# Sliding-window attention and a feed-forward layer on one core: three visits to small matmul tiles in a period instead of four

## The chip, the cores and the metric

The kernel runs on one core of one Trainium2 chip. Its engines work side by side, each through its own queue in order: TensorE (PE in the profile; PEld is its weight loads), VectorE (DVE), ScalarE (ACT), GpSimd (POOL), and SyncE (SP), which issues the DMAs. TensorE writes to PSUM, from where VectorE and ScalarE read. The metric is the time of one execution on the device in microseconds (us).

## What is computed

Attention with 8 heads over 576 positions for 8 batches, where half of the heads see the last 32 positions and half see every fourth of the last 128; its output, 4608 tokens of 512, goes through two matrices with a Gelu between. All data is float32.

```
scores = scale * q @ k.T                      # per batch and head, 576 x 576
mask_plain = (rel >= 0) & (rel < 32)
mask_dil = (rel >= 0) & (rel < 128) & (rel % 4 == 0)
attn = softmax(where(mask, scores, -1e9))     # heads 0-3 plain, heads 4-7 dilated
x = (attn @ v) as (4608, 512)
h = x @ w_in                                  # 512 x 2048
out = gelu(h) @ w_out                         # 2048 x 512
```

## The kernel before

The work is cut into 16 chunks, each half a batch: 288 tokens. A chunk c has four pairs of heads; pairs 0 and 1 are plain, pairs 2 and 3 dilated. The feed-forward products are large: 128 x 128 weights, 288 columns. To keep float32's accuracy in a faster format, each operand is held as a high and a low part (xh and xl, the two halves of win, wout and g), and each product is three matmuls.

Chunks 0 and 1 and the attention of chunk 2 are set in order by a planner (`Plan`), which this change does not touch. From chunk 2 on the order is written out (lines 604 to 653). One chunk's feed-forward is a period of 32 positions. Positions 0 to 15 are the first products: for each of 16 blocks f of the hidden size, 12 matmuls into one PSUM bank (ps_h, line 445), then Gelu and a copy on ScalarE and a residue on VectorE. Positions 16 to 31 are the second products: for each of 4 output blocks d, 16 x 3 matmuls into one bank (ps_o, line 459), then a copy by VectorE and a store. Position 16 + 4d + f/4 stands behind block f of output block d.

Into the period of chunk c-1 the attention of chunk c is sown. Each of its steps has a position and a rank in a table (lines 604 and 605, one entry for each pair); steps are sorted by position, then by rank, then as they were added, and `upto` emits what is due. All engines' queues follow that one order. The steps of a pair are:

- load (A_LOAD): q and k into raw_qk. The products' v comes for all pairs at A_V.
- scores (A_SC, line 310): small float32 matmuls, 64 rows by 32 columns of the array, 18 for a plain pair from here on and 24 for a dilated one, into half of each of two PSUM banks (ps_a).
- lowest (A_SC too, line 322): in three parts u, VectorE adds the mask, takes each row's minimum of the negated scores and moves them to sm.
- softmax (A_E, line 331): in three parts, six exponentials with sums on ScalarE, in place.
- norm and turn (A_N): VectorE divides (lines 352 to 361) and transposes (lines 371 and 376) into the tile turned.
- av and xout (A_X): the products with v (line 411), small matmuls on quarters of the array, 64 x 64, 18 or 24 a pair, into px_a; then ScalarE copies the high part xh (line 431) and VectorE forms the residue xl (line 434), which the next period's first products read.

A "visit" below is a place where TensorE leaves the large matmuls for these small ones. Two pairs share a PSUM tile of two banks, and tiles take turns on four banks (ps_a and px_a, a ring of two). A float32 matmul leaves two records in the trace, and two weight loads.

## Time and profile before

| | |
|---|---|
| median of 3 runs | 946.67 us (945.33 to 946.92) |
| the profiled execution | 945.82 us, span 944.0 us |
| granted TensorE clock, mean | 0.998 |
| TensorE busy | 916.4 us, 97% of the span |
| VectorE busy | 500.2 us, 53% |
| ScalarE busy | 435.4 us, 46% |
| chain that ended last | PE 96%; ps_h 44%, ps_o 44%, px_a 4%, ps_a 3% |

The chain that ended last is followed back from the last instruction, at each step to what released it. With 96% of it on TensorE, the other engines matter where TensorE waits for one of them, and the small matmuls matter by the time that they take TensorE away from the large ones. Matmuls are pipelined: a record lasts longer than the distance to the next one, and its end is modelled.

### The profile page before, as it was taken

The numbers are of one execution on the slowest core, as the hardware profiler recorded it, in microseconds if no ns is written. First come the engines' busy times: TensorE is split into PE (matmuls) and PEld (weight loads), VectorE is DVE, ScalarE is ACT, GpSimd is POOL, SyncE is SP. The second block draws the span as 40 slices with busy tenths as digits, with TensorE's granted clock in tenths as the row PEclk, the third lists the DMA queues.
The fourth block names the chain that finished last, engine by engine and source line by source line (L and its number), as shares of the span: only waits on it lengthen the run. The fifth ranks groups of instructions, "written<-read, shape, count | busy, mean of one in ns | idle before, by whom it ended". The sixth has DMA issues, their size and how long they took to land.

```text
span 944.0 us, 27638 instructions
## 1 busy us (share of the span) xinstructions
PE 916.4 (97%) x11632; PEld 898.6 (95%) x11632; DVE 500.2 (53%) x1957; ACT 435.4 (46%) x1398; POOL 21.0 (2%) x64
## 2 busy tenths in 40 slices
PE   4599999999999999999999999999999999999998
PEld 3499999999999999999999999999999999999998
DVE  6889974364635446354454635446354454635420
ACT  5535453634536245363634546255363634546240
POOL 1400020000000000000000000000000000000000
PEclk9999999999999999999999999999999999999999
DMA  9987233022040401204022040401204022040000
GB/s 319 405 297 261 92 126 137 4 78 75 8 145 8 132 17 51 103 8 145 2 82 71 8 146 8 138 9 60 93 8 145 2 86 68 13 139 8 21 1 26
DMA packets 34988, 83.69 MB, mean 89 GB/s; under 512 B 3888, under 2 KB 12080, under 8 KB 34864
## 3 DMA queue, kind: packets, MB, share of 16 engines
q1 hardware_dynamic: 34864, 81.93, 25.3%
q8 instruction: 91, 1.49, 0.7%
q14 instruction: 33, 0.27, 0.1%
HBM read 72.47 MB, written 9.44 MB: 87 GB/s over the span
## 4 chain that ended last, share of the span: by engine, by line
PE 96%; DMA 1%; issue 1%; DVE 1%; ACT 0%; SPq 0%
PE ps_h L445 44%; PE ps_o L459 44%; PE px_a L411 4%; PE ps_a L310 3%; DMA raw_qk<-qk_d 1%; PE px L395 1%; PE ps_sc L310 1%; DMA raw_w<-w_in 0%; DVE sm L322 0%; PE px L411 0%; DVE cv L199 0%; DVE sm L361 0%; ACT sm L331 0%; DVE cv L197 0%; DVE win L232 0%
## 5 line engine op out<-in xcount | busy, mean ns | idle before, releaser
L459 PE MATMUL ps_o<-g,wout 128*128 128x288 f32 x3072 | 420.1, 296 | 0.0
L459 PEld LDWEIGHTS ps_o<-g,wout 128*128 128x128 f32 x3072 | 409.7, 188 | 0.9
L445 PE MATMUL ps_h<-xh,win 128*128 128x288 f32 x1920 | 388.7, 297 | 0.0
L445 PEld LDWEIGHTS ps_h<-xh,win 128*128 128x128 f32 x1920 | 308.2, 188 | 2.8
L445 PE MATMUL ps_h<-xl,win 128*128 128x288 f32 x960 | 284.0, 296 | 0.0
L454 DVE TENSOR_TENSOR g<-gf,g 128x288 fp32r<-128x288 f32 x256 | 117.0, 457 | 259.2 <-ACT g L452 259.0
L449 ACT ACTIVATE gf<-ps_h 128x288 f32<-128x288 f32 x256 | 105.2, 411 | 297.6 <-PE ps_h L445 297.5
L445 PEld LDWEIGHTS ps_h<-xl,win 128*128 128x128 f32 x960 | 181.0, 189 | 0.0
L331 ACT ACTIVATE sm<-sm,st 128x64 f32<-128x64 f32 (+1 forms) x360 | 120.2, 335 | 12.5 <-DVE st L322 11.4
L452 ACT CAST g<-gf 128x288 fp32r<-128x288 f32 x256 | 111.0, 434 | 7.9
L431 ACT CAST xh<-px_a 128x256 fp32r<-128x256 f32 (+1 forms) x78 | 29.5, 413 | 132.7 <-PE px_a L411 84.8
L376 DVE STREAM_TRANSPOSE turned<-sm 32x192 f32<-32x192 f32 (+2 forms) x248 | 81.3, 328 | 6.2
L179 DVE COPY o_sb<-ps_o 128x288 f32<-128x288 f32 x58 | 26.4, 456 | 83.3 <-PE ps_o L459 82.4
L331 ACT ACTIVATION_READ_ACCUMULATOR sm<-sm,st 128x1 f32 (+1 forms) x360 | 67.2, 187 | 0.0
L434 DVE TENSOR_TENSOR xl<-px_a,xh 128x256 fp32r<-128x256 f32 (+1 forms) x78 | 31.3, 429 | 37.5 <-ACT xh L431 37.1
L322 DVE CUSTOM_DVE_ANT_0 sm<-ps_a,masks 128x64 f32<-128x64 f32 (+1 forms) x312 | 48.0, 216 | 0.6
L371 DVE STREAM_TRANSPOSE turned<-sm 128x256 f32<-128x256 f32 (+2 forms) x90 | 41.1, 457 | 9.0 <-POOL sm L358 4.2
L411 PEld LDWEIGHTS px_a<-turned,v_all 64*64 64x64 f32 x2184 | 35.6, 135 | 4.3 <-issue 4.3
L411 PE MATMUL px_a<-turned,v_all 64*64 64x32 f32 (+1 forms) x2184 | 38.2, 216 | 0.0
L361 DVE TENSOR_TENSOR sm<-sm,st 128x256 f32<-128x256 f32 (+2 forms) x82 | 35.1, 428 | 2.8
L352 DVE TENSOR_SCALAR st<-st 128x4 f32<-128x4 f32 (+2 forms) x90 | 14.2, 160 | 31.0 <-ACT sm L331 30.1
L310 PE MATMUL ps_sc<-raw_qk 64*32 64x64 f32 x504 | 12.3, 294 | 18.8 <-issue 8.4
(40 smaller groups left out, 392.8 us busy)
## 6 DMA issues: line engine op xcount, KB each, us to landing
raw_qk<-qk_d SPq DMA_DIRECT2D x32, 364.0 KB, 5.4
v_all<-v_p SPq DMA_DIRECT2D x28, 384.0 KB, 3.8
v_all<-v_d SPq DMA_DIRECT2D x28, 384.0 KB, 5.4
raw_qk<-qk_p SPq DMA_DIRECT2D x32, 304.0 KB, 4.2
outT<-o_sb SPq DMA_DIRECT2D x64, 144.0 KB, 1.8
raw_w<-w_in SPq DMA_DIRECT2D x16, 512.0 KB, 6.1
raw_w<-w_out SPq DMA_DIRECT2D x16, 512.0 KB, 5.7
mid_w<-w_out SPq DMA_DIRECT2D x10, 511.5 KB, 8.0
```

Of the source, the lines that this page charges most:

```text
L310: nc.tensor.matmul(s.sc[h][32 * r:32 * r + 32, u * 2 * KB:(u + 1) * 2 * KB], x[:, q0:q0 + 32], x[:, k0:k0 + 2 * KB], start=True, stop=True)
L322: nc.vector.tensor_tensor_reduce(out=s.sm[rs, i], in0=s.sc[h][rs, cols], in1=mask_of(s, u), scale=-SCALE, scalar=3.0e38, op0=ALU.add, op1= ...
L331: nc.scalar.activation(t, t, AF.Exp, bias=s.st[rs, 0, i:i + 1], scale=-1.0, accum_out=s.st[rs, 1, i:i + 1])
L361: nc.vector.tensor_mul(t, t, st.unsqueeze(2).broadcast_to((rs.stop - rs.start, 2 * (u1 - u0), 2 * KB)))
L371: nc.vector.transpose(s.t[rs, i].rearrange("p i j b -> p (i j b)"), s.sm[rs, i].rearrange("p i k -> p (i k)"))
L376: nc.vector.transpose(s.t[32 * to:32 * to + 32, i, r % 2], s.sm[32 * r:32 * r + 32, i, j * KB:(j + 1) * KB])
L411: nc.tensor.matmul(px[h * D:(h + 1) * D, r - r0, u * KB:u * KB + b], s.v[rows, u, j, h * D:(h + 1) * D], s.t[rows, 2 * u + h, j, 0:b], sta ...
L445: nc.tensor.matmul(ps, wins[f][:, t, cc * P:(cc + 1) * P], xx, start=(n == 0), stop=(n == 3 * NC - 1))
L449: nc.scalar.activation(gf, ps, AF.Gelu)
L452: nc.scalar.copy(g[:, 0], gf)
L454: nc.vector.tensor_sub(g[:, 1], gf, g[:, 0])
L459: nc.tensor.matmul(ps, wouts[f][:, t, d * P:(d + 1) * P], gs[f][:, u], start=(f == 0 and n == 0), stop=(f == NF - 1 and n == 2))
```

## The change

Two lines of the table, the rule for when a new PSUM tile is taken, the position of a pair's minima and one rank are changed. Scores of pairs 0, 1 and 2 stand at position 3 together, pair 3's at 22.25, behind the products of pairs 0 and 1, which move there from 22.5 and get rank 0. The products of pairs 2 and 3 move from 27 to 28. The minima of pairs 0 to 2 are spread over positions 3 to 11, one part at each; pair 3's follow its scores at once, and its exponentials, normalization and transposes move behind them. Pairs 0 and 1 share a score tile; pairs 2 and 3 take one each.

```diff
-    A_LOAD, A_V, A_SC, A_X = -6, 2, (3, 3, 9, 9), (22.5, 22.5, 27, 27)
-    A_E, A_N = (16.25, 16.5, 16.75, 17), (18.5, 20, 21.5, 23.25)
+    A_LOAD, A_V, A_SC, A_X = -6, 2, (3, 3, 3, 22.25), (22.25, 22.25, 28, 28)
+    A_E, A_N = (16.25, 16.5, 16.75, 22.5), (18.5, 20.25, 22, 25.5)
...
     def scores_of(s):
-        if s.p % 2 == 0:
+        if s.p != 1:
             banks["s"] = ps_a.tile([P, 2, 512], F32, tag="a", name="ps_a")
...
             for u in range(NU):
-                add(A_SC[p], 2, lowest(s, u))
+                add(A_SC[p] + (NU * p + u if p < 3 else 0), 2, lowest(s, u))
                 add(A_E[p], 3, softmax(s, u))
...
-            add(A_X[p], 6, av_of(s))
+            add(A_X[p], 0, av_of(s))
```

On TensorE, the second products of a period before, with the visits of pairs 0 and 1 and of pairs 2 and 3:

```order
L459 MATMUL ps_o<-g,wout 128x288 x81
L411 MATMUL px_a<-turned,v_all 64x32 x36
L459 MATMUL ps_o<-g,wout 128x288 x54
L411 MATMUL px_a<-turned,v_all 64x32 x16
L411 MATMUL px_a<-turned,v_all 64x8 x8
```

The same stretch of TensorE's queue now:

```order
L459 MATMUL ps_o<-g,wout 128x288 x78
L411 MATMUL px_a<-turned,v_all 64x32 x36
L310 MATMUL ps_a<-raw_qk 32x64 x24
L459 MATMUL ps_o<-g,wout 128x288 x69
L411 MATMUL px_a<-turned,v_all 64x32 x16
L411 MATMUL px_a<-turned,v_all 64x8 x8
```

The first of the two visits stands three large matmuls earlier and has pair 3's 24 score matmuls at its end; the second stands 12 further on. Among the first products, where visits of 36 and 48 score matmuls stood, one of 60 stands now, at the place of the first.

On VectorE before, from pair 1's last transposes on (the row of 128 x 384 is a dilated pair's):

```order
L371 STREAM_TRANSPOSE turned<-sm 32x128
L376 STREAM_TRANSPOSE turned<-sm 32x2x32
L352 TENSOR_SCALAR st<-st 128x6
L354 RECIPROCAL st<-st 128x6
L361 TENSOR_TENSOR sm<-sm,st 128x384
L371 STREAM_TRANSPOSE turned<-sm 128x384
L376 STREAM_TRANSPOSE turned<-sm 32x6x32 x4
L434 TENSOR_TENSOR xl<-px_a,xh 128x4x2x32
L434 TENSOR_TENSOR xl<-px_a,xh 128x32
```

VectorE from the same place now:

```order
L371 STREAM_TRANSPOSE turned<-sm 32x128
L376 STREAM_TRANSPOSE turned<-sm 32x2x32
L352 TENSOR_SCALAR st<-st 128x6
L354 RECIPROCAL st<-st 128x6
L361 TENSOR_TENSOR sm<-sm,st 128x384
L371 STREAM_TRANSPOSE turned<-sm 128x384
L376 STREAM_TRANSPOSE turned<-sm 32x6x32 x4
L322 ISA sm,st<-ps_a,masks 128x64
L322 ISA st 128x1
```

Pair 3's six minima (two rows each) have come between pair 2's transposes and the residues of pairs 0 and 1; all that stands ahead of pair 2's transposes is as before.

On ScalarE before, the exponentials of pairs 1 to 3 and the copies of the high parts:

```order
L331 ACTIVATE sm,st<-sm,st 128x64 x12
L431 CAST xh<-px_a 128x4x2x32
L431 CAST xh<-px_a 128x32
L431 CAST xh<-px_a 128x4x2x32
L431 CAST xh<-px_a 128x32
L431 CAST xh<-px_a 128x4x72 x2
```

And now:

```order
L331 ACTIVATE sm,st<-sm,st 128x64 x6
L431 CAST xh<-px_a 128x4x2x32
L431 CAST xh<-px_a 128x32
L431 CAST xh<-px_a 128x4x2x32
L431 CAST xh<-px_a 128x32
L331 ACTIVATE sm,st<-sm,st 128x64 x6
L431 CAST xh<-px_a 128x4x72 x2
```

Pair 3's six exponentials have moved behind the copies of pairs 0 and 1.

## Rows read from the trace of the kernel before

**Rows 1.** Chain of waits in order of time, one period, last chunk: start, length, what
```profile
437.44 6.37 PE ps_h L445 x48
...
444.74 9.75 PE ps_h L445 x72
...
465.37 10.71 PE ps_o L459 x81
476.08 1.30 PE px_a L411 x72
...
484.75 1.51 PE px_a L411 x96
...
494.02 6.37 PE ps_h L445 x48
...
889.80 25.49 PE ps_h L445 x192
```

**Rows 2.** Timeline of TensorE's matmuls at the second visit: start, length, instructions
```profile
454.20 0.29 PE L445 MATMUL ps_h<-xl,win 128*128 128x288 f32 x1
454.42 0.30 PE L310 MATMUL ps_a<-raw_qk 64*32 64x64 f32 x9
...
454.87 0.75 PE L310 MATMUL ps_a<-raw_qk 64*32 64x64 f32 x51
455.55 0.53 PE L445 MATMUL ps_h<-xh,win 128*128 128x288 f32 x2
```

**Rows 3.** Timeline of VectorE: minima of the first visit, pairs 1 and 2
```profile
444.75 0.46 DVE L454 TENSOR_TENSOR g<-gf,g 128x288 fp32r<-128x288 f32 x1 [1.13 <-ACT g L452]
445.13 0.22 DVE L322 CUSTOM_DVE_ANT_0 sm<-ps_a,masks 128x64 f32<-128x64 f32 x1
...
445.27 0.22 DVE L322 CUSTOM_DVE_ANT_0 sm<-ps_a,masks 128x64 f32<-128x64 f32 x1
...
476.78 0.24 DVE L376 STREAM_TRANSPOSE turned<-sm 32x64 f32<-32x64 f32 x1
477.05 0.17 DVE L352 TENSOR_SCALAR st<-st 128x6 f32<-128x6 f32 x1
...
478.69 1.56 DVE L376 STREAM_TRANSPOSE turned<-sm 32x192 f32<-32x192 f32 x4
480.28 0.52 DVE L434 TENSOR_TENSOR xl<-px_a,xh 128x256 fp32r<-128x256 f32 x2
```

**Rows 4.** Timeline of TensorE, third and fourth visit; last its loads by form
```profile
476.01 1.37 PE L411 MATMUL px_a<-turned,v_all 64*64 64x32 f32 x72
...
477.02 0.36 PE L411 MATMUL px_a<-turned,v_all 64*64 64x32 f32 x6
...
477.07 0.20 PEld L411 LDWEIGHTS px_a<-turned,v_all 64*64 64x64 f32 x4
...
477.31 7.44 PE L459 MATMUL ps_o<-g,wout 128*128 128x288 f32 x54
...
484.68 1.49 PEld L411 LDWEIGHTS px_a<-turned,v_all 64*64 64x64 f32 x96 [0.16 <-issue]
...
L411 PEld LDWEIGHTS px_a<-turned,v_all 64*64 64x64 f32 x168 | 2.8, 135 | 0.3 <-issue 0.3
```

**Rows 5.** Timeline of TensorE early in the kernel: products of chunk 0, then scores
```profile
39.38 0.51 PE L395 MATMUL px<-turned,v_sb 32*64 32x32 f32 x27
39.81 0.32 PE L310 MATMUL ps_sc<-raw_qk 64*32 64x64 f32 x8
```

**Rows 6.** ScalarE: timeline of pair 1's copy; exponentials of the period by form
```profile
480.83 0.46 ACT L431 CAST xh<-px_a 128x256 fp32r<-128x256 f32 x2 [2.95 <-DVE xl L434]
...
L331 ACT ACTIVATE sm<-sm,st 128x64 f32<-128x64 f32 x20 | 6.7, 334 | 0.0
```

**Rows 7.** DMA queue in the first period: timeline, then issues by line with time to landing
```profile
156.51 0.91 SPq L262 DMA_DIRECT2D raw_qk<-qk_d  x2
...
raw_qk<-qk_d SPq DMA_DIRECT2D x2, 364.0 KB, 5.4
```

## The prediction

> **What bounds the kernel now.** I read the share of the span by engine first: TensorE is busy for 97% of it and makes up 96% of the chain that ended last (the table above), so only what TensorE does, or waits for, is worth anything. Next I read that chain in order of time [rows 1]. It repeats a period of 56.58 us (437.44 to 494.02), thirteen times up to 889.80, once for the attention of each chunk from 3 to 15: a stretch of first products (ps_h) with two visits to small score tiles, then a stretch of second products (ps_o) with two visits to the attention products (px_a). The last chunk has no visits, and its ps_h stretch of 192 matmuls takes 25.49 us [rows 1], 0.133 us each. In a period the same stretch runs from 437.44 to 465.37, 27.93 us, so the two score visits cost 2.44 us together.

> That cost splits by visit. From 437.44 to 444.74 are 7.30 us, 6.37 of them for 48 large matmuls: 0.93 us. The 72 matmuls behind that visit take 9.75 us, where 72 x 25.49 / 192 is 9.56: they come 0.19 us late. So the first visit costs 1.12 us, and 1.32 are left for the second. Every small matmul leaves two records (fp32): the first visit has 72, the second 96, so 24 more records cost 0.20 us, 8.3 ns each, and a visit without records would still cost about 0.5 us. Within a visit the pace is uneven [rows 2]: the second starts 45 records in its first 0.45 us (454.42 to 454.87), and then 51 between 454.87 and 455.40 (end of the row less the 0.22 us that one lasts), 10.6 ns each.

> The third visit is already late in the kernel before. VectorE ends pair 1's last transpose at 477.02 (476.78 + 0.24) and goes on with pair 2 at 477.05 [rows 3]; the last four weight loads of pair 1's product begin at 477.07 [rows 4], 0.05 us behind it. In the fourth visit 96 loads take 1.49 us and one lasts 0.135 [rows 4]: 14.3 ns from one start to the next; at that pace the four would have begun 68 loads after 476.01, at 476.98. So the end of the third visit is set by VectorE and not by TensorE.

> **The change, part by part.**

> *Fewer visits among the first products.* The second visit goes, and pair 2's 48 records join the first. One visit of 120 records costs 1.52 us by the difference between visits (1.32 + 24 x 0.0083) and 1.63 us if the 48 run at the later pace (1.12 + 48 x 0.0106). I take 1.60, since records that join a running visit meet the later pace. The gain is 2.44 - 1.60 = 0.84 us a period, bounds 0.81 and 0.92.

> *Products of pairs 0 and 1 three matmuls earlier.* At 22.25 in place of 22.5, 78 large matmuls of the stretch are done and not 81. TensorE reaches the visit 3 x 0.133 = 0.40 us earlier, but what ends the visit is VectorE's transpose, and nothing moves that. In the order on VectorE the whole row from pair 0's normalization to pair 1's transposes, the first output copy between them, is the same, and ScalarE's softmax of pairs 0 and 1 is too; both start behind the last Gelu, which stands at a fixed distance from the start of the ps_o stretch. So the av matmuls end where they ended, and the three matmuls that used to lie under the wait come after it: a loss of 0.40 us a period. It would be a gain of nothing, and a loss of nothing, only if pair 1's transposes came 0.4 us sooner.

> *Pair 3's scores behind these products.* In the kernel before, the large matmuls resume at 477.31, which is 0.07 us ahead of the modelled end (477.02 + 0.36) of the last small one [rows 4]. The same 0.07 us shows where a visit begins (454.20 + 0.29 against 454.42 [rows 2]), and 0.08 us at a change from one small shape to another without a large one between, at the start of the kernel: 39.38 + 0.51 against 39.81 [rows 5]. So I start the scores at 477.31, as the large matmuls before. Their 48 records take some 0.48 us to start by the head of [rows 2] (bounds 0.40 and 0.51, at 8.3 and 10.6 ns), the last one ends 0.22 us on, and the large matmuls begin 0.07 us ahead of that: 477.93, 0.62 us later than before. If the change of shape cost nothing, the scores would begin some 0.13 us sooner; if it cost what a visit's beginning does (0.22 us from the start of the last matmul, [rows 2], against 0.15 here), 0.07 us later. [...] With a free change inside the visit the sum below would be +0.05 us a period in place of +0.18.

> *Sum for a period:* + 0.62 (scores of pair 3 here) + 0.40 (the three matmuls) - 0.84 (two visits into one) = +0.18 us. The bounds: 0.81 - 0.92 = -0.11 and 1.12 - 0.81 = +0.31 us (0.81 is 1.02 less 0.13 and 0.08, 1.12 is 1.02 plus 0.07 and 0.03).

> *VectorE's score minima spread over nine steps.* The bursts of twelve among the ps_h stretch become nine pieces of two. I cost it at nothing: VectorE idles 1.13 us ahead of a residue in that stretch, and two minima take 0.29 us (0.145 us apart, [rows 3]). If that cover were gone, Gelu would wait for its buffer and TensorE for a PSUM bank; shorter pieces make this less likely than before.

> *Pair 3's chain gets late.* Its minima, exponentials and transposes now lie between its scores and the last visit. VectorE is busy with pair 2 until 480.25 (478.69 + 1.56), and then, where it started pair 0's residue at 480.28 [rows 3], it takes six minima: 0.87 us, to 481.15. Pair 0's residue follows (0.52 us, to 481.67), and it alone lets ScalarE copy pair 1, as it did at 480.83, 0.03 us after that residue [rows 6]: 481.70 to 482.16. Behind that copy in ScalarE's queue stand pair 3's six exponentials, 334 ns each [rows 6]: to about 484.3 with the last read-out. Behind VectorE's wait for them stand the normalization and the transposes, 3.20 us as pair 2's (477.05 to 480.25): to 487.5. TensorE needs them when? From 477.93, 69 large matmuls take 9.36 us (69 x 0.1328 and 0.19), so the last visit begins at 487.3; pair 2 goes first with 48 records at 14.3 ns, 0.7 us: 488.0. The chain has some 0.5 us in hand, so I cost it at nothing. Residues of pairs 2 and 3, the output copies and the reload of Gelu's table end some microseconds ahead of the next ps_h stretch, which follows 45 matmuls (6 us) behind that visit.

> *Loads.* The order of the DMA queue does not change, and pair 3's tile is held for longer without a load that waits for it. Only in the first period are the loads issued close ahead: pairs 2 and 3 from 156.51, and they land 5.4 us later in the median [rows 7], at 161.9. The first visit reached its end at about 161.8; pair 2's scores now stand there. That may cost 0.2 us, once.

> **The time.** 13 x 0.18 = 2.3 us, with 0.2 for the load not added: the profiled execution of 945.82 us (span 944.04) becomes 948.2. It lies 0.85 us below the median of the runs, 946.67; carried over to that median the sum is 949.0 us. Bounds: 13 x -0.11 = -1.4 and 13 x 0.31 = +4.0, thus 945.2 to 950.7.

> **Rivals.**
> 1. *The visit saved is a plain gain.* If VectorE's transpose of pair 1 did not end the merged visit, the 0.40 would fall away and the period would be 0.22 us shorter: 13 x 0.22 = 2.9 us, 943.8 us. For it: a visit does cost 0.5 us however small it is. Against it: the 0.05 us between transpose and loads in [rows 3, 4], and an order on VectorE and ScalarE that is the same up to there. It decides from the point at which the transpose ends before about 476.6. 8%.
> 2. *Gain and loss cancel.* The change of shape costs little, the 48 records run at 8.3 ns in both places, and the sum lies between -0.11 and +0.05 us: about 946.3 us. For it: the records of small matmuls come in bursts, and [rows 5] are from the start of the kernel and another shape. 26%.
> 3. *Pair 3 comes late to the last visit.* Its chain runs through three engines with 0.5 us in hand; 0.9 us more on it would stop TensorE 0.4 us in each period, 5 us more than my sum: 954 us. For it: every link waits for another engine. Against it: every link has a duration from the trace. 7%.

> My forecast, a sum from +0.05 to +0.31 us a period, has 59%, and its own range is 947.3 to 950.7. With the cancelling case and some of the scatter of the runs (945.33 to 946.92), the range is 945.4 to 951.0. About 0.2%, 1.9 us, is what a measurement can tell from no change here. The forecast is beyond that from 0.15 us a period on, some four fifths of its chance: with rival 3, 54% slower; 8% faster; 38% for no change.

> **What would show it.** In the profile of the changed kernel: a ps_h stretch of about 27.1 us with one visit; a third-visit row in which the last four loads of pair 1's product still begin 0.05 us behind VectorE's transpose, about 11.8 us after the stretch's start, although the visit begins 0.4 us earlier; the scores starting 0.15 us behind the last product; large matmuls again 0.6 us later; and a last visit without a gap. The period should be 56.76 us. I am wrong if the merged visit ends earlier than VectorE lets it by this reading, if one visit of 120 records costs far from 1.6 us, or if TensorE idles in the last visit.

## The result, and the profile after

The changed kernel takes 949.79 us, median of 8 runs (948.45 to 952.09), against 945.52 us for the kernel before (8 runs, 944.74 to 948.31). The ratio is 1.0041, with a 95% interval of 1.0031 to 1.0051: slower by 0.41%, 2.9 to 4.8 us. The forecast was 949.0 us in a range of 945.4 to 951.0, slower, by a sum of 2.3 us. The runs of one kernel spread with the granted clock of TensorE, so equal clocks are compared too: at 0.998 the changed kernel takes 948.45 to 950.00 us (median of three 948.58), at 0.996 949.18 to 949.94 (949.63), at 0.994 951.62 and 952.09. The kernel before, in its runs beside the experiments below on two chips, has medians of 945.67 (34 runs), 946.23 (9) and 948.61 (5) at these clocks. That is 2.9 to 3.4 us less at each.

The chain of waits of the changed kernel in order of time (start, length, what); a period from 441.10 to 497.92 answers to [rows 1]:

```profile
157.11 6.37 PE ps_h L445 x48
...
441.10 6.38 PE ps_h L445 x48
447.48 1.44 PE ps_a L310 x92
448.92 19.31 PE ps_h L445 x144
468.23 10.31 PE ps_o L459 x78
478.54 1.36 PE px_a L411 x66
...
480.24 0.66 PE ps_a L310 x45
480.89 9.36 PE ps_o L459 x69
490.26 1.51 PE px_a L411 x96
491.77 6.15 PE ps_o L459 x45
497.92 6.37 PE ps_h L445 x48
...
895.59 25.49 PE ps_h L445 x192
```

Read it by stretches. From 441.10 to 468.23 are 27.13 us, where the kernel before has 27.93: 0.80 us are gained by one score visit in place of two, with pair 3's 48 records gone to the merged visit. From 468.23 to 480.89 are 12.66 us for 78 large matmuls and the merged visit; before, 81 large matmuls and the visit took 12.01 us (465.37 to 476.08 + 1.30). So the large matmuls resume 0.65 us later, and with three of them (0.40 us) still to do. The last visit takes 1.51 us as before. Sum: 0.65 + 0.40 - 0.80 = +0.25 us.

Over all thirteen periods, from the start of the first to the start of the last chunk's first products, it is 895.59 - 157.11 = 738.48 us. The kernel before starts them here, in its own chain:

```profile
154.66 6.37 PE ps_h L445 x48
```

889.80 - 154.66 = 735.14 us. The periods are 3.34 us longer, 0.26 each, which lies inside the interval of the runs. The span of this one profiled execution grew by more, 5.8 us (949.8 against 944.0): the other 2.45 us lie ahead of the first period, where both kernels have the same instructions in the same order. There the granted clock was at 0.50, with 1.00 ahead of it and behind it, from 47.38 to 57.62 us in this execution, and from 48.80 to 52.21 in that of the kernel before. Twelve large matmuls took 3.18 us at 0.50 (from 48.61) and 1.59 at 1.00 (from 62.11). TensorE was busy for 4.01 of the 6.83 us ahead of the one fall and for 6.30 of the 10.24 us ahead of the other. By its length the difference, 6.8 us more at half the pace, can hold the 2.45 us, but two other profiles with 3.41 us at the lower clock begin the first period at 153.91 and 155.25, so it need not be the clock alone. That start ended between 153.91 and 157.11 us in the profiles of kernels that share it, so comparisons below are made by the thirteen periods and by the runs, not by spans.

VectorE in the changed kernel (start, length, instruction): the end of pair 1's transposes, the second of the two residues of pairs 0 and 1, then pair 3's normalization and transposes:

```profile
479.64 0.24 DVE L376 STREAM_TRANSPOSE turned<-sm 32x64 f32<-32x64 f32 x1
...
485.00 0.52 DVE L434 TENSOR_TENSOR xl<-px_a,xh 128x256 fp32r<-128x256 f32 x2 [0.53 <-ACT xh L431]
...
486.99 0.17 DVE L352 TENSOR_SCALAR st<-st 128x6 f32<-128x6 f32 x1 [1.10 <-ACT sm L331]
...
488.62 1.55 DVE L376 STREAM_TRANSPOSE turned<-sm 32x192 f32<-32x192 f32 x4
```

TensorE's matmuls and loads in the same two visits:

```profile
478.47 1.77 PE L411 MATMUL px_a<-turned,v_all 64*64 64x32 f32 x72
...
479.93 0.30 PE L411 MATMUL px_a<-turned,v_all 64*64 64x32 f32 x4
480.17 0.34 PE L310 MATMUL ps_a<-raw_qk 64*32 64x64 f32 x16
...
490.18 1.49 PEld L411 LDWEIGHTS px_a<-turned,v_all 64*64 64x64 f32 x96 [0.17 <-issue]
```

Three things are to be seen. The 72 product records take 1.77 us where they took 1.37 [rows 4]: the visit begins 0.40 us earlier and does not end earlier. The last four begin at 479.93, 0.05 us behind VectorE's transpose (479.64 + 0.24), the distance of [rows 3, 4]. And the transpose ends 11.65 us behind the start of the ps_o stretch (479.88 - 468.23), as before (477.02 - 465.37). The granted clock was 0.994 over the span, 0.998 before; within the periods the large matmuls kept their pace (25.49 us for 192 in both).

### The profile page after: what moved, and what is told of

Same layout as the page of the kernel before. It is cut to its first block, busy times and chain, and to the rows that moved or that the text cites. A ratio compares the mean times of both kernels' runs of the same rounds, so it can differ in the third digit from the quotient of the medians.

```text
span 949.8 us, 27626 instructions
## 1 busy us (share of the span) xinstructions
PE 922.3 (97%) x11632; PEld 903.9 (95%) x11632; DVE 501.8 (53%) x1957; ACT 435.7 (46%) x1398; POOL 21.1 (2%) x64
## 3 DMA queue, kind: packets, MB, share of 16 engines
q8 instruction: 91, 1.49, 0.7%
## 4 chain that ended last, share of the span: by engine, by line
PE 96%; DMA 2%; issue 1%; DVE 0%; SPq 0%
PE ps_h L445 44%; PE ps_o L459 43%; PE px_a L411 4%; PE ps_a L310 3%; DMA raw_qk<-qk_d 1%; DMA mid_w<-w_out 1%; PE px L395 1%; DMA v_sb<-v_p 1%; PE ps_sc L310 0%; PE px L411 0%; DVE sm L322 0%; SPq L262 0%; DVE cv L199 0%; DVE o_sb L179 0%; DVE raw_w L203 0%
## 5 line engine op out<-in xcount | busy, mean ns | idle before, releaser
L322 DVE CUSTOM_DVE_ANT_0 sm<-ps_a,masks 128x64 f32<-128x64 f32 (+1 forms) x312 | 54.8, 219 | 1.0
L411 PEld LDWEIGHTS px_a<-turned,v_all 64*64 64x64 f32 x2184 | 37.7, 134 | 7.2 <-issue 4.2
L411 PE MATMUL px_a<-turned,v_all 64*64 64x32 f32 (+1 forms) x2184 | 42.9, 217 | 0.4
L322 DVE DVE_READ_ACCUMULATOR2_ANT st<- 128x1 f32 (+2 forms) x384 | 31.3, 81 | 0.0
```

The costliest lines, as they stand in the source:

```text
L322: nc.vector.tensor_tensor_reduce(out=s.sm[rs, i], in0=s.sc[h][rs, cols], in1=mask_of(s, u), scale=-SCALE, scalar=3.0e38, op0=ALU.add, op1= ...
L411: nc.tensor.matmul(px[h * D:(h + 1) * D, r - r0, u * KB:u * KB + b], s.v[rows, u, j, h * D:(h + 1) * D], s.t[rows, 2 * u + h, j, 0:b], sta ...
```

## Experiments

All ratios are to the kernel before, timed on the same chip.

**Scores first in the merged visit.** One rank of the changed kernel is put back.

```diff
-            add(A_X[p], 0, av_of(s))
+            add(A_X[p], 6, av_of(s))
```

> The changed kernel with one rank put back: in the merged visit at 22.25 pair 3's scores come ahead of the products of pairs 0 and 1, so TensorE works on them while VectorE ends pair 1's transposes. Theory (the loss is 0.40 us a period of waiting for that transpose, beside 0.66 us for pair 3's scores here, against 0.80 us saved among the first products): the scores fill the wait, the products end about 12.1 us after the start of the second products in place of 11.95, and a period is 0.25 us shorter than that of the kernel before: 13 x 0.25 = 3.3 us faster than before, some 6.6 us faster than the changed kernel. Rival (two shapes in one visit, or scores in that place, are what costs): the order inside the visit makes no difference, and it stays 3 to 4 us slower than before.

Measured: 943.56 us, ratio 0.9972 (0.9960 to 0.9983), 1.6 to 3.8 us faster than before. TensorE's matmuls in its merged visit, the second products having begun at 463.56:

```profile
473.83 0.72 PE L310 MATMUL ps_a<-raw_qk 64*32 64x64 f32 x48
474.49 1.25 PE L411 MATMUL px_a<-turned,v_all 64*64 64x32 f32 x72
475.67 0.40 PE L459 MATMUL ps_o<-g,wout 128*128 128x288 f32 x1
```

The products take 1.25 us in place of 1.77: their wait lies under the scores now. The thirteen periods take 732.57 us, 2.57 less than before. Twelve of them are 56.27 to 56.33 us long, 0.25 less than the 56.55 before, as expected; the one that begins at 717.93 takes 56.95, because TensorE stands still for 0.39 us ("issue") a few matmuls behind its score visit; the last section has the reason. The rival that the order inside the visit makes no difference is out: the same instructions in another order turn the loss into a gain. Of all versions run this is the fastest.

**Products three matmuls earlier, nothing else.** The kernel before with one number changed:

```diff
-(22.5, 22.5, 27, 27)
+(22.25, 22.25, 27, 27)
```

> The kernel before with one number changed: the products of pairs 0 and 1 at 22.25 in place of 22.5, three large matmuls earlier; four visits as before. Theory: the visit begins 0.40 us earlier and ends where it ended, since VectorE's transpose of pair 1 sets its end: 13 x 0.40 = 5.2 us slower than before. Rival (TensorE does not wait there, the visit takes its time whatever VectorE does): no change, within 1 us of before.

Measured: 950.51 us, ratio 1.0047 (1.0031 to 1.0063). Its chain of waits shows the visit in two pieces:

```profile
466.50 10.31 PE ps_o L459 x78
476.81 1.36 PE px_a L411 x66
...
478.20 0.30 PE px_a L411 x4
478.51 7.73 PE ps_o L459 x57
```

From 476.81 to 478.51 are 1.70 us where [rows 1] have 1.30: the 0.40 us that the visit came earlier. VectorE's last transpose of pair 1 there:

```profile
477.91 0.24 DVE L376 STREAM_TRANSPOSE turned<-sm 32x64 f32<-32x64 f32 x1
```

It ends at 478.15, and the last four records begin at 478.20. The thirteen periods are 4.95 us longer than before (740.09), 0.38 each. So this part of the change, alone, costs more than the whole of it (3.34).

**The merged visit at 22.5.** The changed kernel with the visit where the products stood before:

```diff
-(3, 3, 3, 22.25), (22.25, 22.25, 28, 28)
+(3, 3, 3, 22.5), (22.5, 22.5, 28, 28)
-(16.25, 16.5, 16.75, 22.5)
+(16.25, 16.5, 16.75, 22.75)
```

> The changed kernel with the merged visit one block later, at 22.5 where the kernel before had its products (pair 3's exponentials at 22.75). Theory: the 0.40 us of added waiting falls away, the scores behind the products stay: -0.80 + 0.66 = -0.14 us a period, 1.9 us faster than before; pair 3's transposes still end some 0.3 us ahead of their use in the last visit. Rival (the place of pair 3's scores behind the products is the loss): still 3 us slower than before. If pair 3's chain came late in the last visit, between the two.

Measured: 944.83 us, ratio 0.9988 (0.9976 to 0.9999); the periods take 733.25 us, 1.89 less than before, 0.145 each. So the scores behind the products cost 0.65 us and no more, and the quarter of a position is what made the change a loss.

**Minima spread, nothing else.**

```diff
-                add(A_SC[p], 2, lowest(s, u))
+                add(A_SC[p] + NU * (p % 2) + u, 2, lowest(s, u))
```

> The kernel before with one part of the change alone: the minima of pairs 0 and 1 spread over positions 3 to 8, those of pairs 2 and 3 over 9 to 14. Theory: VectorE idles there, nothing waits for it: within 1 us of before, and the stretch of first products stays 27.93 us. Rival (spreading delays Gelu's buffers or wakes VectorE at a worse time): 1 us or more slower, which would be a share of the change's loss.

Measured: 946.23 us, ratio 0.9999 (0.9989 to 1.0009), periods 735.29 us: nothing, as costed. The minima are spread here behind each of the two score visits, six steps each, and not over nine steps behind one.

**The last visit at 27.** The changed kernel with its last visit 12 large matmuls earlier.

```diff
-(22.25, 22.25, 28, 28)
+(22.25, 22.25, 27, 27)
```

> The changed kernel with the last visit back at 27, 12 large matmuls earlier. Theory: in the changed kernel pair 3's transposes end about 0.7 us ahead of their use; 1.6 us earlier they are late by 0.8 to 0.9 us in each period: 10 to 12 us slower than the changed kernel, 14 to 16 slower than before. Rival (pair 3's chain runs behind TensorE and has more in hand, or TensorE's wait moves VectorE forward): same as the changed kernel, 4 us slower than before.

Measured: 960.20 us, ratio 1.0156 (1.0141 to 1.0171). Its weight loads in the last visit stop twice for VectorE:

```profile
490.34 0.90 PEld L411 LDWEIGHTS px_a<-turned,v_all 64*64 64x64 f32 x52 [0.16 <-issue]
491.63 0.21 PEld L411 LDWEIGHTS px_a<-turned,v_all 64*64 64x64 f32 x8 [0.39 <-DVE turned L376]
492.03 0.66 PEld L411 LDWEIGHTS px_a<-turned,v_all 64*64 64x64 f32 x36 [0.20 <-DVE turned L376]
```

The thirteen periods take 749.55 us, 0.85 each more than in the changed kernel, as expected. So pair 3's chain does become the bound once it is 1.6 us less ahead, as the third rival has it; at 28 it is not.

**One visit for all scores.** The saving part of the change alone, driven further: 168 records in one visit, minima spread.

```diff
-(3, 3, 9, 9)
+(3, 3, 3, 3)
```

> The kernel before with the scores of all four pairs at position 3 (168 records in one visit), their minima spread over positions 3 to 14, products where they were. It does the saving part of the change alone. Theory: one visit of 120 records cost 1.64 us of the first products; 48 more at 10.6 ns make it 2.15, against 2.44 for two visits: 13 x 0.29 = 3.8 us faster than before. Rival (a visit has no cost of its own, small matmuls cost by their number): within 1 us of before.

Measured: 951.85 us, ratio 1.0058 (1.0041 to 1.0076): the expectation missed by some 9 us. Its chain of waits in two neighbouring periods:

```profile
389.62 1.92 PE ps_a L310 x119
391.54 19.33 PE ps_h L445 x144
...
445.82 1.86 PE ps_a L310 x116
447.68 1.38 issue
449.06 0.31 PE ps_a L310 x5
```

The first is what was expected (the shortest period is 56.19 us, 0.35 less than the usual one before). In the second TensorE stands still inside the visit, and "issue" says that it waits for nothing that the profile shows. This happens in six of the thirteen periods, for 0.3 to 1.7 us, inside the visit or a few matmuls behind it.

**One visit for all products; two visits a period.** The kernel before with all products at 28, first with its two score visits (the edit shown), then with one score visit and spread minima as well.

```diff
-(22.5, 22.5, 27, 27)
+(28, 28, 28, 28)
```

> The kernel before with the products of all four pairs in one visit at 28; the score visits and minima as before. Three visits a period, by another way than the change. Theory (a visit has some 0.5 us of its own, and the late transpose of pair 1 no longer ends one): 3.20 us for two product visits become 2.75: 13 x 0.45 = 5.9 us faster than before, about 940. If 168 product records in a row outran the instruction supply as 168 score records did, some 1.5 us more in every second period: 4 us slower than before. Rival (a late visit leaves the copies and residues of four pairs to the next first products): a gap at the start of the first products, slower.

> The kernel before with two visits a period: the scores of all pairs at 3, their minima spread, and the products of all pairs at 28. Where the one visit of 168 score records was not interrupted, a period was 0.35 us shorter than before; one visit of 168 product records should cost 1.71 + 72 x 0.0145 = 2.75 us in place of 3.20 (the 0.1 us of waiting among them gone). Theory A (a large visit can outrun the supply of TensorE's instructions, 336 of them in 1.8 us; the stall comes where a 16 KB instruction fetch comes late): some score visits stall 1.4 to 1.9 us, the slower product visits hardly; gain 13 x 0.80 = 10.4 us less 5 to 10 us of stalls: 936 to 946 us. Theory B (the stall of the score visit came from something else in that kernel, as the spread minima or the loads): no reason to stall here less or more than there, the product visit is free of it. Read from stalls by visit.

Measured: 956.77 us, ratio 1.0117 (1.0097 to 1.0137), and 962.12 us, ratio 1.0175 (1.0152 to 1.0197). Both gains that were expected (to about 940 us, and to 936 to 946) are missed. The undisturbed periods of the first are 56.06 to 56.14 us long, 0.45 less than before, as expected. The others are longer by up to 6.1 us. TensorE in one of these, in the kernel with one product visit:

```profile
259.30 0.95 PE L411 MATMUL px_a<-turned,v_all 64*64 64x8 f32 x49
...
263.69 0.39 PE L411 MATMUL px_a<-turned,v_all 64*64 64x8 f32 x6 [3.43 <-issue]
```

The stall is not all of the loss. From 262.31 to 269.14, and again from 436.39 to 443.22 in and behind the next stall, the granted clock was at 0.50, where the rest of the periods had 1.00. TensorE had stood still from 260.26 on when it fell first, and from 435.06 on the second time. The stretch from the end of the stall to the end of the low clock (start and end, length, busy time and instructions of PE, PEld, DVE, ACT and POOL, granted clock, DMA share, GB/s):

```profile
263.69:269.14 5.45, 5.45 (x27) 5.43 (x28) 1.36 (x2) 2.63 (x3) 0.00 (x0) 0.50 0.04 16
```

In the second stretch the chain has 44 large matmuls in 8.62 us from 437.61 on, where 44 x 25.49 / 192 is 5.84: 2.78 us more, half of the 5.61 us up to 443.22. By the same share, half of 5.45 us and the 3.43 us of the stall make about the 6.1 us by which this period is longer.

Of the theories on record for the stalls, the one that the spread minima made them is out, since this kernel has them without.

**The loads moved away.** Tried three times: q and k at 19 of the period ahead (for the product visit), v at 6 (for the score visit), both (for two visits).

```diff
-A_LOAD, A_V, A_SC, A_X = -6, 2, (3, 3, 9, 9), (28, 28, 28, 28)
+A_LOAD, A_V, A_SC, A_X = -13, 2, (3, 3, 9, 9), (28, 28, 28, 28)
...
-A_LOAD, A_V, A_SC, A_X = -6, 2, (3, 3, 3, 3), (22.5, 22.5, 27, 27)
+A_LOAD, A_V, A_SC, A_X = -6, 6, (3, 3, 3, 3), (22.5, 22.5, 27, 27)
...
+A_LOAD, A_V, A_SC, A_X = -13, 6, (3, 3, 3, 3), (28, 28, 28, 28)
```

> The kernel with one product visit at 28, and the loads of q and k moved from position 26 of the period ahead to 19, so that they are done when the visit begins. Theory A (the stalls of a large visit are a 16 KB fetch of TensorE's instructions that comes behind the bulk loads on the same DMA engines): the stalls of 0.7 to 3.6 us disappear or shrink below 0.5, and the kernel comes to what its undisturbed periods show, 56.10 us: 13 x 0.45 = 5.9 us faster than before. Theory B (336 instructions in a row outrun the supply by themselves): the stalls stay, and it is again about 1.2% slower than before.

> The kernel with one score visit at 3 and spread minima, and the loads of v moved from position 2, just ahead of that visit, to 6, behind it. Theory A (instruction fetch behind the bulk loads): the stalls of 1.1 to 1.9 us disappear, and with 56.20 us a period it is 13 x 0.35 = 4.5 us faster than before. Theory B (the pace of the score matmuls alone, 5.3 ns an instruction, outruns the supply): again some 0.6% slower than before, with the same stalls.

> Two visits a period with both loads moved: q and k at 19 of the period ahead, v at 6. Theory A: a period of 55.75 us without stalls, 13 x 0.80 = 10.4 us faster than before, some 935 us, ahead of both kernels. Theory B: stalls of up to 3 us in half of the periods, some 1.7% slower than before as the two visits were with the loads beside them.

Measured: 947.84 us, ratio 1.0017 (1.0005 to 1.0029); 952.99 us, ratio 1.0070 (1.0059 to 1.0082); 957.23 us, ratio 1.0109 (1.0094 to 1.0125). The first missed its 5.9 us of gain, but it shortened the stalls of the product visit, five of up to 3.4 us, to three of up to 1.5 us, and the two stretches at the lower clock from 6.8 us to 3.4 us each. The same place as in the fence above, with the loads away:

```profile
259.08 1.66 PE L411 MATMUL px_a<-turned,v_all 64*64 64x32 f32 x98
...
262.20 0.29 PE L411 MATMUL px_a<-turned,v_all 64*64 64x8 f32 x6 [1.46 <-issue]
```

It stops six records ahead of the end in both, for 3.43 and 1.46 us. The second experiment did not do what it was to do. The DMA queue waited for no position here: v is issued at the same point of the period, in the kernel with v at 2 and in that with v at 6:

```profile
440.40 0.88 SPq L269 DMA_DIRECT2D v_all<-v_p  x2
```

```profile
439.97 0.88 SPq L269 DMA_DIRECT2D v_all<-v_p  x2
```

So it says nothing on whether v's loads lengthen the score visit's stalls, and neither does the third. But the third moved the loads of q and k from the product visit to the score visit. They are issued 2.8 us into the period (440.26), ahead of the score visit at 446.63:

```profile
443.08 4.46 SPq L262 DMA_DIRECT2D raw_qk<-qk_p  x2
```

Against the two visits without that move, the stalls of the product visits fell from 8.9 us in sum over the profile to 3.8, and those of the score visits rose from 7.7 to 11.0. So the stalls were longer in the visit that the loads of q and k lay beside, and some remained without them (3.8 us in the product visits).

## Why the prediction was right

*TensorE bounds the kernel, and the third visit was late already.* Right. The last loads follow the transpose by 0.05 us in the kernel before, in the changed one and with the products early, though the visit begins 0.4 us apart. They begin 11.70 us behind the start of the stretch, now as before ("about 11.8" in the forecast, but 477.07 - 465.37 is 11.70).

*Two score visits into one gain 0.84 us.* They gain 0.80: the visit of 120 records costs 27.13 - 25.49 = 1.64 us in place of the 1.60 taken, the upper bound of the two readings (1.63). Here the records that joined the visit were paid at its late pace.

*The products three matmuls earlier lose 0.40 us.* Right, and shown alone: 0.38 us a period.

*Pair 3's scores there cost 0.62 us.* 0.65, by the chain and by the visit at 22.5. The change of shape inside the visit was sized right: the scores begin at 480.17, 0.06 us ahead of the modelled end of the last product (479.93 + 0.30), where 0.07 was taken.

*Sum: +0.18 us a period.* It is +0.26: the two sizes above are 0.04 and 0.03 low, both in the same direction. Thirteen periods make 3.34 us in place of 2.3. The median moved by 4.3, with an interval that holds 3.34, and at equal granted clock the kernels are 2.9 to 3.4 us apart; the rest may lie in which clocks the eight runs of each met, which is on record for the changed kernel's alone.

*The time of 949.0 us.* It came within 0.8 us of the measured 949.79 by luck. It started from a median of 946.67 us, of three runs, which eight runs put at 945.52; that is 1.15 us too high, and the step that was added, 2.3 us, was 2.0 too low against the median's.

*Spread minima cost nothing.* Right, by the experiment with them alone.

*Pair 3's chain has 0.5 us in hand.* It has 0.7: the transposes end at 490.17, and pair 3's records, the second half of the visit's 96, begin at about 490.88 (490.18 + 48 x 0.0145, an estimate). The order of steps was as argued, and ScalarE shows it:

```profile
484.50 0.46 ACT L431 CAST xh<-px_a 128x256 fp32r<-128x256 f32 x2 [3.76 <-DVE xl L434]
484.85 0.36 ACT L331 ACTIVATE sm<-sm,st 128x64 f32<-128x64 f32 x1
```

Pair 1's copy waited 3.76 us for VectorE, and pair 3's exponentials stood behind it. The forecast's 0.2 us for the loads in the first period did not show: that visit is as long as the others.

*The rivals.* The plain gain would have needed a visit whose end VectorE does not set; putting the scores first makes just that, and the gain is there (2.57 us by the periods, and 0.25 in each undisturbed one, where the rival had 0.22). Gain and loss did not cancel. The late chain of pair 3 is real, but 0.7 us away.

## What to carry to other kernels

Merging small stretches of work into fewer visits saved a price for each here: 0.35 us in the undisturbed periods with one score visit, 0.45 with one product visit, and 0.25 where scores and products share a visit with the scores first. But the place of the merged visit must be read against whoever supplies it: the one here ended on another engine's result, gained nothing from beginning 0.40 us earlier, and the three matmuls pulled out from under the wait were paid in full (0.38 us a period). Inside such a visit put the work that waits for nothing first. And a visit can grow too large: at 120 small matmul records there was no stall in the changed kernel and one of 0.39 us with the scores first; at 168 there were stalls larger than the saving.

## What the runs showed of the hardware that was not expected

Visits of 168 small matmul records stopped TensorE for "issue", for up to 3.43 us. These visits are 336 instructions with their weight loads, and the stalls stand at the same records in kernels that share the stretch: in the score visits at records 156, 163, 125 and 132, with v at 2 or at 6, and in the product visits at 162 and 145, with the loads beside them or away. They come at the same points of the instruction stream, and not when some other engine is late.

The trace points to what they are, since it holds the packets of a queue that it calls instruction. That queue reads, in the page of the kernel with one score visit as in that of the kernel before (packets, MB, share):

```profile
q8 instruction: 91, 1.49, 0.7%
```

```profile
q8 instruction: 1, 0.02, 6.2%
```

It began 0.46 us behind the start of the stall, beside the loads, and took 1.53 us; with the loads away the packet for the same record began 0.87 us ahead of the stall (259.87) and took 1.10, and TensorE went on at 262.20. So by these positions and times TensorE waited there for its own instructions, and longer beside the loads (3.43 us) than without them (1.46). Large matmuls use up 256 instructions in 17 us (128 x 0.133), score records in 1.1 to 1.4 us (128 at 8.3 to 10.6 ns), by estimate; the 91 packets of the kernel before took 0.88 to 1.72 us, and TensorE went on 1.2 us or more behind one. No run took the fetch away or made it earlier, so the cause rests on these positions and times.
